# Weighted values two groups behind, two rings of weighted scores, and row maxima sent and fetched in separate groups, in an attention and MLP kernel

## The chip, the cores and the metric

The kernel runs on one core of a Trainium2 chip. The metric is the device time of one execution in microseconds. Before the change it is 1613.96 us, the median of three runs (1613.82 to 1614.4). One execution was profiled: it took 1613.86 us, and its span on the engines, from the first instruction to the last, is 1612.1 us.

## The reference

The input is 2048 rows of 512 numbers. A layer norm, attention with 32 heads of 16 columns each, a projection, a residual; then a second layer norm and an MLP of width 1792 with SiLU, and a residual again:

```python
scores = jnp.einsum("bhqd,bhkd->bhqk", q, k) * scale
p = _softmax(scores, axis=-1)
o = jnp.einsum("bhqk,bhkd->bhqd", p, v)
...
h = x + _A_ref(_layernorm(x, axis=-1), A_wqkv, A_wo)
h2 = h + _B_ref(_layernorm(h, axis=-1), B_w1, B_w2)
```

## The kernel before

**Stages.** Until about 180 us the kernel normalizes the rows and makes queries, keys and values. Then comes the attention as one long loop (line 1392), and after it, from about 1500 us, the end of the last block's MLP. The 2048 query rows are four blocks of 512. An *item* is four heads of one block, 32 items in all, and has 16 *groups*; a group takes 128 keys for the four heads, so there are 512 groups.

**A group.** For each of its four heads (numbered k = 0 to 3) TensorE makes scores of 128 keys by 512 queries in PSUM (`ps<-qs,ks`), ScalarE weighs them, which is the exponential, into an SBUF tile of the pool `bp` (`pt<-ps`, L111), and TensorE multiplies the values into them (`ps<-pt,va`, function `values`): four matmuls of 17 columns side by side in the array, each as two instructions since the tiles are float32, so eight instructions, a *burst* in this text. The four sums lie in one PSUM bank, `pv`. When the 16 groups of an item are summed, `finish_item` (line 881) has ScalarE copy the bank out (`pvs`, for items from 8 on) before the next item's first burst may write it, and starts a chain of DMAs and GpSimd work that divides by the sums.

**Maxima.** The softmax needs each row's maximum beforehand. A *maximum* is one matmul of 128 queries by 512 keys (`ps<-ks,qs`) and one VectorE reduction of 512 columns (`mx<-ps`, L307). Sixty-four of them make an item complete. The maxima run ahead of the scores by a plan, `maxima(g)` at line 1361, which says how many fall into each group. `at["done"]` counts those issued.

**What becomes of finished maxima.** `found_maxima` (line 399) chooses. If the item's scores begin more than FAR = 5 groups later, GpSimd reduces the rest and three ticks later (a tick, line 384, is the start of a group) `place_far` (line 344) has VectorE transpose the result (`mt<-ns`) and issues six DMAs on SyncE's queue: four that send it to DRAM (`md<-mt`) and two that fetch it back as two rows of the query tile (`qs<-md`), which wait for the four. Otherwise the late way is taken: VectorE and GpSimd reduce at once, and two groups later `place_max` (line 357) transposes on TensorE, copies on VectorE and issues two DMAs (`qs<-mn`). In such a group one maximum fewer is planned. The scores of an item read these rows, so they wait for the DMA.

**The two kinds of group.** For three of the four blocks the MLP of the block before is computed beside the attention: after the items 8, 16 and 24 begin, some groups hold the output projection, the second layer norm and its transpose (function `output`, line 1224), and then 112 groups in a row (the last time 110) are *beside* groups. These are the groups 146 to 257, 274 to 385 and 402 to 511. In the transpose, four tiles `g` of two buffers are filled by ScalarE and GpSimd or VectorE, and each is sent by a transposing DMA on SyncE's queue (`hts<-g`, line 131).

In a beside group, `beside_products` (line 1178) interleaves half-height matmuls of the MLP (64 of 128 rows) with the group's scores and maxima on the other 64 rows, so that two run at once. It works on pairs of groups: in the even group G it makes the scores of the heads k = 0 and 2 of both G and G+1, and in the odd group G+1 those of k = 1 and 3 of both. Six halves are done in a group. When a chain of halves is complete, always in an odd group, ScalarE copies its bank out (`g<-ps,factors`), between the second and the third exponential. In beside groups three PSUM banks take turns for scores (four otherwise) and three for maxima.

**Lag.** At the end of group g the values of group g - 2 are multiplied in, but in beside groups those of group g - 1 (line 1464: `while done <= g - (1 if g in beside else LAG)`). All weighted scores share one ring of 12 tiles. Every engine runs its instructions in the order in which this program issues them, DMAs of SyncE's queue included.

**Plan in beside groups.** Four maxima are planned in a beside group, five while `64 + 4 * (g + LEAD) > at["done"]` with LEAD = 7 (3 in the last 110), line 1368.

Of the kernel before, what the change touches and what calls it, by code (L numbers as in the profile page):

```python
# [10 lines left out]
F32 = mybir.dt.float32  # L11
# [9 lines left out]
P = 128  # L21
# [6 lines left out]
FC = F // P  # L28
# [18 lines left out]


LAG = 2
PTS = 12  # L50

RING = 5

# [20 lines left out]

LOOK = 5

LEAD = 7


BESIDE_V = [(0, 0), (0, 0, 4, 4)], [(2, 4), (4, 4, 4, 4)], [(6, 6), (6, 6, 6, 6)]  # L80
# [9 lines left out]
def attention_mlp_kernel(ctx: ExitStack, tc: tile.TileContext, x, wqkv, wo, w1, w2, out):  # L90
# [253 lines left out]
    def place_far(piece):  # L344

        i, _ = piece
        mt = small.tile([P, 32], F16, name="mt")
        dve("transpose", mt, split.pop(piece))
        issue = dma
        for b in range(4):  # L350
            issue(md[i, :, 32 * b:32 * b + 32], mt[32 * b:32 * b + 32, :])
        for j in range(2):
            issue(qs[i % RING][64 * j + 48:64 * j + 50].rearrange("r a n -> r (a n)"),
                md[i, 16 * j:16 * j + 16, :].rearrange("(r q) n -> r (q n)", r=2))
        placed.add(piece)

    def place_max(piece):

# [99 lines left out]

    groups = ITEMS * KC
    pts, den = {}, {}  # L460

    def pt_tile(name, dtype=F32):
        return bp.tile([P, 512], dtype, tag="pt", name=name)

    def scores(g, k, kind="st"):

        i = g // KC
        a, j, c = head(g, k)
        assert piece_of(i, a) in placed
        ps = bank(kind)  # L470
        mm(ps, ks[i % RING][64 * j:64 * j + 64, a, c * P:(c + 1) * P], qs[i % RING][64 * j:64 * j + 64, a, :],
           start=True, stop=True)

        def weigh():
            pts[g, k] = pt_tile("pt")
            return act("activation", pts[g, k], ps, AF.Exp, scale=qk_f)

        return weigh
# [117 lines left out]
    def project_qk(b, n, beside={}, scale=False):  # L596

        g, key = divmod(n, 2)
        cols = slice(key * D + g * P, key * D + (g + 1) * P)
        ps = bank()  # L600
        if b == 0 and g == 0:
            cols = slice(key * P, (key + 1) * P)
            wh, wl, xh, xl = wqk0_h, wqk0_l, xth0, xtl0
        else:
            wh, wl, xh, xl = wqk_h, wqk_l, xth[b], xtl[b]
        weave(product(ps, lambda c: wh[:, c, cols], lambda c: wl[:, c, cols],
                      lambda c: xh[:, c, :], lambda c: xl[:, c, :], DC),
              {k: n if callable(n) else (lambda n=n: burst(n)) for k, n in beside.items()})
        sh = xp.tile([P, 512], F16, name="sh")
        sl = xp.tile([P, 512], F16, name="sl", bufs=2)  # L610
        if scale:

            t = scaled[b % 2]
            act("mul", t, ps, 1 / (16.0 * LN))
            act("copy", sh, t)
            pool("tensor_tensor", sl, t, sh, ALU.subtract)
        else:
            act("mul", sh, ps, qk_0)
            dve("scalar_tensor_tensor", sl, ps, qk_0, sh, op0=ALU.mult, op1=ALU.subtract)
        d = (kd if key else qd)[g * P:(g + 1) * P, :, b * 512:b * 512 + 512]  # L620
        hs, ls = (slice(0, 3, 2), 1) if key else (slice(0, 2), 2)
        dma(d[:, hs], sh[:, None, :].to_broadcast([P, 2, 512]))
        dma(d[:, ls], sl)
# [185 lines left out]

    pb.close()  # L810
    cpool = ctx.enter_context(tc.tile_pool(name="cpool", bufs=1, side="right"))
    bp = ctx.enter_context(tc.tile_pool(name="bp", bufs=PTS, side="right"))
    first_scores = [(g, m ^ (g % 2)) for g in range(LAG) for m in range(4)]

    def begin_scores(n):
# [15 lines left out]
    for g in range(1, NG // 2):  # L831
        for m, (b, key) in enumerate([(b, 1) for b in range(NB)] + [(b, 0) for b in range(NB)]):
            tick()
            if g == 1 and m < 2:
                fixed_rows(2 + m)
            n = 8 * g + m - 12
            square_rest(n + 24)
            if n == 15:
                measure_rest()
            if n == 18:  # L840
                set_factors()
            beside = {BESIDE_A1[m]: 6} if g == 1 and m < len(BESIDE_A1) else BESIDE_A
            if n >= 18:
                beside = BESIDE_T[n - 18]
            project_qk(b, 2 * g + key, beside, True)
            for load, i, h in loads.get(n, ()):
                load(i, h)
    pa.close()
# [141 lines left out]
    def parts_of(w):  # L990
        return w.bitcast(F16).rearrange("p (s n) -> p s n", s=2)
# [69 lines left out]
        low(halves[t][:, 1], rows, halves[t][:, 0], "pool" if t < 3 else "dve")  # L1061

    def gate(ps, engine="dve"):
        g, parts = zp.tile([P, 512], F32, name="g"), parts_of(pt_tile("gh"))
        act("activation", g, ps, AF.Silu, scale=h_f)
        act("mul", parts[:, 0], g, g_s)
        if engine == "pool":
            pool("tensor_scalar", g, g, g_s, 1.0, op0=ALU.mult, op1=ALU.mult)
            low(parts[:, 1], g, parts[:, 0], "pool")
        else:  # L1070
            dve("scalar_tensor_tensor", parts[:, 1], g, g_s, parts[:, 0], op0=ALU.mult, op1=ALU.subtract)
        return parts[:, 0], parts[:, 1]
# [178 lines left out]
    def finish_last(pending):  # L1251
# [85 lines left out]
        for f in range(FC):  # L1337
# [11 lines left out]
            if f > 1:  # L1349
                second(b, acc, *waiting.pop(0))  # L1350
        last_seconds(b, acc, [gate for _, *gate in waiting])

    marks = [KC * (8 * b + 1) for b in range(1, NB)]

    beside = {g for m in marks for g in range(m + 2, min(groups, m + 2 + 4 * FC + 4 * FC))}
    fixed = {**{8 * KC * b + c: 3 + (MORE[c - OUTPUT - 1] if OUTPUT < c <= OUTPUT + 4 else 0) for b in range(1, NB) for c in range(2, KC + 2)},
             **{g: 4 for g in beside}}
    before = [sum(n for x, n in fixed.items() if x < g) for g in range(groups + 1)]
    free = [sum(x not in fixed for x in range(g)) for g in range(groups + 1)]

    def maxima(g):

        i, c = divmod(g, KC)
# [28 lines left out]
    for g in range(groups):  # L1392
        tick()
        i, c = divmod(g, KC)
        at["group"], at["next"] = None, g
        if g in marks:
            begin_mlp(i // 8 - 1)
        if (g in beside) != (g - 1 in beside):
            lay_out(st=range(3 if g in beside else 4))
        if i + RING - 1 < ITEMS and 6 <= c < 14:  # L1400
            (load_k if c % 2 else load_q)(i + RING - 1, c // 2 - 3)
        if g < DC:
            w = raw_tile()
            dma(w, wo[g * P:(g + 1) * P, :])
            soon(8, split_wo, g, w)
        f, c4 = divmod(g - SPLIT, SPACING)
        if c4 == 0 and 0 <= f < 2 * FC:
            kind, f = ("w1", "w2")[f % 2], f // 2
            soon(4, split_weights, kind, f, load_raw(kind, f))
        if i in FIRSTS:  # L1410
            b, n = i // 8 - 1, c - OUTPUT
            if c < 4:
                load_rows(b, c)
            if c == 9:
                wanted.extend(weights_of)
                if i == FIRSTS[-1]:
                    wanted.extend((("w1", 0), ("w1", 1), ("w1", 2), ("w2", 0)))
            if c in (9, 12, 13, 14, 15):
                want(1)
            if c in (3, 4):  # L1420

                split_rows(b, c - 3, slice(0, DC - 1))
            if n == 0:
                for t in range(2):
                    split_rows(b, t, slice(DC - 1, DC))
        if i == LAST:
            if c < 4:
                load_rows(NB - 1, c)
            if 5 <= c < 9:

                split_early(c - 5)
        if g == 1:
            dve("memset", pv, 0.0)
        at["group"] = g
        n = maxima(g)

        if g in beside:
            beside_products(g, n)
        else:
            half = 1 - head(g, g % 2)[1]  # L1440
            j = next_item()
            more = len(todo[j, half]) - len(todo[j, 1 - half]) if j < ITEMS else 0
            slots = range(n)
            if n == 3 and more < 0:
                slots = range(1, 4)
            if n == 2 and more > 0:
                slots = 0, 2
            for m in range(4):
                k = m ^ (g % 2)
                if (g, k) not in pts:  # L1450
                    scores(g, k)()
                if m in slots:
                    one_max(1 - head(g, k)[1])
        if found_at["step"] < at["step"]:
            finish_rest()
        for j in late.pop(at["step"], ()):

            place_max(j)
        if i in FIRSTS and OUTPUT + 1 < c < OUTPUT + 4:

            split_rows(i // 8 - 1, c - OUTPUT)
        if i in FIRSTS and c > OUTPUT:
            output(i // 8 - 1, c - OUTPUT - 1)
        while done <= g - (1 if g in beside else LAG):
            values(done)
            done += 1
    assert at["done"] == END
# [33 lines left out]
```

## Time and profile before

| what | value |
|---|---|
| median of three runs | 1613.96 us (1613.82 to 1614.4) |
| profiled execution | 1613.86 us, span 1612.1 us |
| TensorE granted clock | 0.993 of full speed |
| TensorE busy | 1586.0 us, 98% |
| VectorE busy | 1377.2 us, 85% |
| ScalarE busy | 1240.0 us, 77% |
| GpSimd busy | 577.8 us, 36% |

PE is TensorE's matmuls, PEld its weight loads, DVE is VectorE, ACT ScalarE, POOL GpSimd, SP SyncE; a q behind the name is the engine's own sequencer, which issues DMAs. Times are microseconds from the start of the span. A tile is written `out<-in`. In the list of instructions in order of time, the columns are start, length, engine, line, operation, tiles, shapes and count; in brackets stands how long the engine was idle before it and what ended that. The chain of waits is followed back from the last instruction and printed as start, length, what. In the table by stretch, a row has the stretch, its length, and the busy time and count of PE, PEld, DVE, ACT and POOL. The ends of matmuls are modelled, so the starts are what is read here.

### The profile page before, as it was taken

What the parts mean: (1) busy time and instruction counts of PE and PEld (TensorE: products, weight loads), DVE (VectorE), ACT (ScalarE), POOL (GpSimd) and SP (SyncE); (2) the same over time, 40 slices, a digit from 0 to 9 for tenths busy, and PEclk for the clock granted to TensorE, in tenths of its full rate; (3) what the DMA queues carried; (4) which work ended last, traced back from release to release, by engine and by line L of the source; (5) the groups of instructions that cost most, each with busy time, mean ns of one, the idle gap of its engine ahead of it and who ended that gap; (6) DMA issues with size and microseconds to landing.
All of it is one profiled execution on the core that took longest, in us unless ns stands there. A gap on an engine that the chain in (4) does not pass through costs nothing.

```text
span 1612.1 us, 31239 instructions
## 1 busy us (share of the span) xinstructions
PE 1586.0 (98%) x11485; PEld 520.1 (32%) x11485; DVE 1377.2 (85%) x2199; ACT 1240.0 (77%) x2404; POOL 577.8 (36%) x861
## 2 busy tenths in 40 slices
PE   9999999999999999999998999999999999999999
PEld 6434222222222333333322333333322333332354
DVE  7999999999998999999887999999887989995232
ACT  5545799999976888877776888877767888778632
POOL 6743544454342454311252454311252444212100
PEclk9999999999999999999999999999999999999999
DMA  6666433334223111444333211444333221334322
GB/s 217 169 179 213 132 85 87 108 113 116 85 62 89 54 49 42 127 133 130 105 73 88 54 47 48 127 128 131 104 79 88 65 58 36 87 102 143 118 82 76
DMA packets 136045, 162.49 MB, mean 101 GB/s; under 512 B 42992, under 2 KB 79920, under 8 KB 135892
## 3 DMA queue, kind: packets, MB, share of 16 engines
q1 hardware_dynamic: 131140, 151.98, 33.7%
q10 hardware_dynamic: 4752, 8.52, 1.9%
q8 instruction: 90, 1.47, 0.4%
q14 instruction: 63, 0.52, 0.1%
HBM read 126.69 MB, written 24.84 MB: 94 GB/s over the span
## 4 chain that ended last, share of the span: by engine, by line
PE 88%; DVE 8%; ACT 1%; DMA 1%; issue 1%; POOL 0%; SPq 0%; POOLq 0%; ACTq 0%; DVEq 0%
PE ps L97 87%; DVE mx L307 6%; DVE mx L305 1%; PE ps L100 1%; ACT pt L111 1%; DMA hts<-g 1%; ACT g L111 0%; POOL wv_l L104 0%; DMA w<-w2d 0%; SPq L127 0%; DVE pvs L121 0%; DVE g L121 0%; DVE st L121 0%; DVE ot L121 0%; DVE ks L121 0%
## 5 line engine op out<-in xcount | busy, mean ns | idle before, releaser
L307 DVE TENSOR_REDUCE mx<-ps 128x1 f32<-128x512 f32 x1842 | 1146.5, 683 | 96.7 <-PE ps L97 72.8
L111 ACT ACTIVATE pt<-ps 128x512 f32<-128x512 f32 x2048 | 1053.7, 605 | 208.9 <-PE ps L97 201.2
L97 PE MATMUL ps<-ks,qs 48*128 48x512 f16 x2048 | 680.4, 382 | 7.6 <-DVE mx L307 4.0
L97 PE MATMUL ps<-qs,ks 64*128 64x512 f16 x2048 | 644.4, 380 | 11.8 <-ACT pt L111 11.7
L97 PE MATMUL ps<-pt,va 128*17 128x512 f32 x4096 | 565.5, 601 | 0.5 <-DVE pvs L121 0.3
L97 PE MATMUL ps<-hts,w 64*128 64x512 f16 (+2 forms) x1212 | 285.1, 372 | 0.3
L97 PE MATMUL ps<-w,gates 64*128 64x512 f16 x1008 | 246.0, 378 | 0.3
L97 PEld LDWEIGHTS <-ks 64*128 64x128 f16 x2048 | 177.5, 95 | 212.5 <-issue 170.1
L97 PEld LDWEIGHTS <-qs 48*128 48x128 f16 x2048 | 169.2, 95 | 78.3 <-issue 35.3
L97 PEld LDWEIGHTS <-w 64*128 64x128 f16 (+1 forms) x1212 | 102.0, 95 | 236.8 <-ACT pt L111 105.6
L104 POOL TENSOR_TENSOR ri<-rc,minus 128x16 f32<-128x16 f32 x31 | 90.7, 2926 | 204.4 <-DMA rc<-dn 204.4
L97 PEld LDWEIGHTS ps<-pt,va 128*17 128x17 f32 x4096 | 84.5, 95 | 221.3 <-issue 207.5
L97 PEld LDWEIGHTS <-gates 64*128 64x128 f16 x1008 | 82.1, 94 | 218.4 <-ACT pt L111 119.7
L305 DVE TENSOR_REDUCE mx<-ps 128x2 f32<-128x1024 f32 x103 | 119.2, 1218 | 4.1 <-PE ps L97 3.5
L104 POOL TENSOR_SCALAR t<-t,factors 128x512 f32<-128x512 f32 x42 | 29.0, 691 | 198.7 <-ACT t L111 198.7
L111 ACT ACTIVATE g<-ps,factors 128x512 f32<-128x512 f32 x68 | 46.9, 690 | 42.6 <-PE ps L97 42.6
L104 POOL TENSOR_TENSOR ot<-ot,g 128x512 f32<-128x512 f32 x12 | 15.2, 1266 | 162.5 <-ACT g L111 162.5
L111 ACT ACTIVATE ks<-ps 128x512 f32<-128x512 f32 x30 | 17.9, 597 | 48.9 <-PE ps L97 43.0
L121 DVE SCALAR_TENSOR_TENSOR gh<-g,factors,gh 128x512 f16<-128x512 f32 x14 | 10.5, 752 | 52.1 <-ACT gh L111 52.1
L104 POOL TENSOR_TENSOR t<-t,g 128x512 f32<-128x512 f32 x42 | 53.5, 1275 | 3.5
L104 POOL TENSOR_TENSOR sl<-ks,sh 128x512 f16<-128x512 f32 x30 | 34.6, 1156 | 50.5 <-ACT sh L111 35.7
L104 POOL TENSOR_TENSOR mx<-mx 128x32 f32<-128x32 f32 x52 | 12.4, 239 | 109.2 <-DVE mx L307 102.6
(161 smaller groups left out, 1065.9 us busy)
## 6 DMA issues: line engine op xcount, KB each, us to landing
w<-w2d SPq DMA_DIRECT2D x182, 256.0 KB
ks<-kd SPq DMA_DIRECT2D x120, 192.0 KB
w<-w1d SPq DMA_DIRECT2D x56, 256.0 KB
ks<-in_B_w_dram ACTq DMA_DIRECT2D x28, 256.0 KB
w<-in_B_w_dram SPq DMA_DIRECT2D x28, 256.0 KB
qs<-qd SPq DMA_DIRECT2D x128, 48.0 KB
kd<-sh SPq DMA_DIRECT2D x16, 256.0 KB
qd<-sh SPq DMA_DIRECT2D x16, 256.0 KB
```

The costliest lines, as they stand in the source:

```text
L97: return tc.keep_in_program_order(nc.tensor.matmul(*a, **k))
L100: tc.keep_in_program_order(nc.tensor.transpose(*a))
L104: tc.keep_in_program_order(getattr(nc.gpsimd, op)(*a, **k))
L111: ins = getattr(nc.scalar, fn)(*a, **k)
L121: pin(getattr(nc.vector, fn)(*a, **k))
L305: pin(nc.vector.tensor_reduce(of, space[:, n:n + 2, :], axis=AX.X, op=ALU.max))
L307: pin(nc.vector.tensor_reduce(of[:, j:j + 1], space[:, n, :], axis=AX.X, op=ALU.max))
```

## The change

At the end of every group the values of two groups earlier are multiplied in, in beside groups too. The ring of 12 tiles becomes two rings, of 6 and 8 tiles; a tile comes from the second ring for odd groups where the group is a beside group, and for the heads k = 2 and 3 elsewhere. LEAD goes from 7 to 5. The four DMAs that send the maxima go out one group after the transpose, and the two that fetch them back one group after that; only ahead of the attention do they still follow at once. The plan's tables (`marks`, `beside`, `fixed`, `before`, `free`) move up in the file so that `scores` can use `beside`, and a local name is changed from `beside` to `bursts`.

```diff
 LAG = 2
-PTS = 12
+PTS = 6, 8
...
-LEAD = 7
+LEAD = 5
...
@@ place_far
         dve("transpose", mt, split.pop(piece))
-        issue = dma
-        for b in range(4):
-            issue(md[i, :, 32 * b:32 * b + 32], mt[32 * b:32 * b + 32, :])
-        for j in range(2):
-            issue(qs[i % RING][64 * j + 48:64 * j + 50].rearrange("r a n -> r (a n)"),
-                md[i, 16 * j:16 * j + 16, :].rearrange("(r q) n -> r (q n)", r=2))
-        placed.add(piece)
+
+        def out():
+            for b in range(4):
+                dma(md[i, :, 32 * b:32 * b + 32], mt[32 * b:32 * b + 32, :])
+
+        def back():
+            for j in range(2):
+                dma(qs[i % RING][64 * j + 48:64 * j + 50].rearrange("r a n -> r (a n)"),
+                    md[i, 16 * j:16 * j + 16, :].rearrange("(r q) n -> r (q n)", r=2))
+            placed.add(piece)
+
+        if at["attention"]:
+            soon(1, out)
+            soon(2, back)
+        else:
+            out()
+            back()
...
-    def pt_tile(name, dtype=F32):
-        return bp.tile([P, 512], dtype, tag="pt", name=name)
+    def pt_tile(name, second, dtype=F32):
+        return bp.tile([P, 512], dtype, tag=f"pt{second}", name=name, bufs=PTS[second])
...
         def weigh():
-            pts[g, k] = pt_tile("pt")
+            pts[g, k] = pt_tile("pt", g % 2 if g in beside else k // 2)
             return act("activation", pts[g, k], ps, AF.Exp, scale=qk_f)
...
     def gate(ps, engine="dve"):
-        g, parts = zp.tile([P, 512], F32, name="g"), parts_of(pt_tile("gh"))
+        g, parts = zp.tile([P, 512], F32, name="g"), parts_of(pt_tile("gh", 1))
...
-        while done <= g - (1 if g in beside else LAG):
+        while done <= g - LAG:
             values(done)
             done += 1
```

More of the change, by code (lines that the diff above doesn't have):

```diff
@@ L460, in attention_mlp_kernel @@
     pts, den = {}, {}
-    def pt_tile(name, dtype=F32):
-        return bp.tile([P, 512], dtype, tag="pt", name=name)
+    marks = [KC * (8 * b + 1) for b in range(1, NB)]
+    beside = {g for m in marks for g in range(m + 2, min(groups, m + 2 + 4 * FC + 4 * FC))}
+    fixed = {**{8 * KC * b + c: 3 + (MORE[c - OUTPUT - 1] if OUTPUT < c <= OUTPUT + 4 else 0) for b in range(1, NB) for c in range(2, KC + 2)},
+             **{g: 4 for g in beside}}
+    before = [sum(n for x, n in fixed.items() if x < g) for g in range(groups + 1)]
+    free = [sum(x not in fixed for x in range(g)) for g in range(groups + 1)]
+    def pt_tile(name, second, dtype=F32):
+        return bp.tile([P, 512], dtype, tag=f"pt{second}", name=name, bufs=PTS[second])
     def scores(g, k, kind="st"):
@@ L811, in attention_mlp_kernel @@
     cpool = ctx.enter_context(tc.tile_pool(name="cpool", bufs=1, side="right"))
-    bp = ctx.enter_context(tc.tile_pool(name="bp", bufs=PTS, side="right"))
+    bp = ctx.enter_context(tc.tile_pool(name="bp", bufs=1, side="right"))
     first_scores = [(g, m ^ (g % 2)) for g in range(LAG) for m in range(4)]
@@ L841, in attention_mlp_kernel @@
                 set_factors()
-            beside = {BESIDE_A1[m]: 6} if g == 1 and m < len(BESIDE_A1) else BESIDE_A
+            bursts = {BESIDE_A1[m]: 6} if g == 1 and m < len(BESIDE_A1) else BESIDE_A
             if n >= 18:
-                beside = BESIDE_T[n - 18]
-            project_qk(b, 2 * g + key, beside, True)
+                bursts = BESIDE_T[n - 18]
+            project_qk(b, 2 * g + key, bursts, True)
             for load, i, h in loads.get(n, ()):
@@ L1351, in finish_last @@
         last_seconds(b, acc, [gate for _, *gate in waiting])
[L1353 to L1359, printed above, removed]
     def maxima(g):
```

## The prediction

> **What bounds the kernel now.** First the page: who is busy, and who ends the chain of waits.
>
> ```profile
> span 1612.1 us, 31239 instructions
> PE 1586.0 (98%) x11485; PEld 520.1 (32%) x11485; DVE 1377.2 (85%) x2199; ACT 1240.0 (77%) x2404; POOL 577.8 (36%) x861
> PE 88%; DVE 8%; ACT 1%; DMA 1%; issue 1%; POOL 0%; SPq 0%; POOLq 0%; ACTq 0%; DVEq 0%
> ```
>
> TensorE's order sets the end; VectorE does for 8%. A TensorE that is busy 98% seems to leave nothing to win. But ends of matmuls are modelled, so a matmul that is held back looks busy. Second, therefore, the matmuls of the values alone, by stretch (first plain groups, then the three runs of beside groups), and third two bursts of eight in order of time with the exponential that ran there.
>
> ```profile
> 181.00:444.00 263.00, 134.52 (x1024) 16.87 (x1016) 0.00 (x0) 0.00 (x0) 0.00 (x0) 1.00 0.37 104
> 499.95:804.60 304.65, 124.95 (x891) 20.18 (x888) 0.00 (x0) 0.00 (x0) 0.00 (x0) 1.00 0.32 90
> 862.30:1167.00 304.70, 125.01 (x892) 20.18 (x888) 0.00 (x0) 0.00 (x0) 0.00 (x0) 1.00 0.32 90
> 1223.00:1500.00 277.00, 114.94 (x824) 18.42 (x816) 0.00 (x0) 0.00 (x0) 0.00 (x0) 1.00 0.30 86
> ...
> 699.82 0.59 ACT L111 ACTIVATE pt<-ps 128x512 f32<-128x512 f32 x1
> 700.28 1.22 PE L97 MATMUL ps<-pt,va 128*17 128x512 f32 x8
> 701.43 0.39 PE L97 MATMUL ps<-w,gates 64*128 64x512 f16 x1
> 702.75 0.37 PE L97 MATMUL ps<-qs,ks 64*128 64x512 f16 x1
> 703.06 1.05 PE L97 MATMUL ps<-pt,va 128*17 128x512 f32 x8
> 704.04 0.39 PE L97 MATMUL ps<-w,gates 64*128 64x512 f16 x1
> ```
>
> Eight matmuls take 134.52 / 128 = 1.051 us where values follow two groups behind. In the three beside runs they take 124.95 / 111.4 = 1.122, 125.01 / 111.5 = 1.121 and 114.94 / 103 = 1.116. The single bursts say why: 1.05 in one group, 1.22 in the other. The long one stands at the end of an odd group, where the even group's values are taken. It needs the exponentials of k = 1 and 3, made in that same odd group, and the one at 699.82 ends at 700.41, after the burst began at 700.28. To the next matmul it is 701.43 - 700.28 = 1.15 us, against 704.04 - 703.06 = 0.98. So 0.17 us of waiting for ScalarE, drawn as busy, is in nearly every second beside group.
>
> **The change part by part.** *Values two behind.* At the end of group G+1 the values of G-1 are then taken, whose exponentials ended a group earlier. All bursts should take 1.05: saved are 111.4 x 0.071 + 111.5 x 0.070 + 103 x 0.065 = 22.4 us, and about 0.7 for the last dozen groups: **-23.1**. The sum of matmuls is the same; the tail has two bursts instead of one behind the last group.
>
> *Two rings.* When the even group's exponentials of k = 0 and 2 are written, the first ring holds four tiles of G-2 and these two: six. In the odd group the second holds four of G-1 and four of G+1: eight. Six and eight are just enough, and the burst that frees a tile stands ahead of the score whose exponential fills it: 0.
>
> *The copy of the sums.* `finish_item` moves from the end of the even group 16n to the end of the odd group 16n+1, and its copy on ScalarE now stands between the exponentials of that group and the next. ScalarE around group 177 (from 584.98 to 587.82):
>
> ```profile
> 585.11 0.58 ACT L111 COPY pvs<-ps 128x512 f32<-128x512 f32 x1
> 585.72 1.08 ACT L111 ACTIVATE pt<-ps 128x512 f32<-128x512 f32 x2
> 586.69 0.69 ACT L111 ACTIVATE g<-ps,factors 128x512 f32<-128x512 f32 x1
> 587.26 2.79 ACT L111 ACTIVATE pt<-ps 128x512 f32<-128x512 f32 x5
> ...
> 702.08 2.08 ACT L111 ACTIVATE pt<-ps 128x512 f32<-128x512 f32 x4 [0.69 <-PE ps L97]
> ```
>
> The odd group also holds the copy of a finished MLP chain (0.69). Its exponentials start at 0.74, 1.2, 2.28 and 2.75 after the group's start; the last ends at 3.37. The copy of 0.6 then ends at 3.97, while the next group's first exponential is due at 2.63 + 0.65 = 3.28 (702.08 - 701.43 = 0.65): 0.69 late. The fourth score of a group reuses the first one's bank, of three: it stands 702.75 - 701.43 = 1.32 after the start, and the first exponential ends at 1.25, so 0.07 is to spare and 0.62 is lost. Chains of the first MLP product end every fourth group, which meets 16n+1 in groups 161, 177, 193 and their like in each run, nine times: **+5.6**. Without the chain's copy the lateness is about 0.09 and the loss 0.02, nine times: **+0.2**. From both sides: 0 if PSUM's turns absorb it, 11 if all 18 lose the 0.62. I take the row's reading. Where a beside run ends (groups 257 and 385) the copy falls among exponentials that TensorE already waits for:
>
> ```profile
> 804.10 1.10 ACT L111 ACTIVATE pt<-ps 128x512 f32<-128x512 f32 x2
> 805.24 0.39 PE L97 MATMUL ps<-qs,ks 64*128 64x512 f16 x2 [0.52 <-ACT pt L111]
> ```
>
> It adds its 0.6 twice: **+1.2** (0 to 1.2).
>
> *LEAD from 7 to 5.* A group with five maxima is bound by VectorE:
>
> ```profile
> 500.36 3.08 DVE mx L307 x5
> 498.00:804.00 306.00, 305.11 (x2467) 100.69 (x2467) 282.65 (x462) 250.56 (x483) 100.75 (x153) 1.00 0.32 90
> ```
>
> It takes 3.08 us against 704.04 - 701.43 = 2.61 with four. I followed line 1368 through all groups by hand: groups with five were 11, 11 and 5 in the three runs and become 2, 13 and 9, since eight maxima fewer are done ahead and the next run starts with that debt. Three fewer: 3 x 0.47 = **-1.4**. The items 17, 18 and 25 are now complete five groups or fewer ahead (groups 267, 283, 395) and take the late way.
>
> *Maxima sent and fetched later.* SyncE's queue and the chain of waits where the second layer norm is transposed:
>
> ```profile
> 837.80 1.16 POOL L104 TENSOR_TENSOR g<-w,g 128x512 f16<-128x512 f32 x1 [0.46 <-ACT g L111]
> 840.70 1.84 DVE L307 TENSOR_REDUCE mx<-ps 128x1 f32<-128x512 f32 x3
> 840.80 2.44 SPq L127 DMA_DIRECT2D md<-mt  x4
> 844.30 0.52 SPq L127 DMA_DIRECT2D qs<-md  x2
> 845.69 1.25 SPq L131 DMA_TRANSPOSE hts<-g  x1
> 845.69 3.89 DMA hts<-g
> 849.66 0.62 ACT L111 CAST g<-w 128x512 f16<-128x512 f32 x1 [5.22 <-DMA hts<-g]
> 850.83 0.58 PE L97 MATMUL ps<-qs,ks 64*128 64x512 f16 x1 [4.41 <-ACT pt L111]
> ...
> 1212.60 0.58 PE L97 MATMUL ps<-qs,ks 64*128 64x512 f16 x1 [3.76 <-ACT pt L111]
> ...
> 479.18 0.32 SPq L127
> 480.47 1.42 DMA md<-mt
> 483.42 3.60 DMA hts<-g
> 488.27 0.58 PE L97 MATMUL ps<-qs,ks 64*128 64x512 f16 x1 [2.49 <-ACT pt L111]
> ```
>
> The second transposing DMA has its tile at 838.96 but stands in SyncE's queue behind the maxima's six DMAs, and goes at 845.69. ScalarE's next `g` waits for it to land, the exponentials queue behind that, and TensorE idles 4.41 us. In the second and third such place (items 17 and 25) the late way now puts two DMAs there, behind a small VectorE copy after two reductions: 840.70 + 1.23 + 0.15 = 842.1, two issues 0.52, so the transpose goes at 842.6, 3.1 us earlier; the third place the same, less its shorter queue, 2.9. In the first (item 9) send and fetch move behind the transposes of the next group. The transpose then goes at 477.4 and the old stall is gone, but the fetch stands behind the last transpose, whose tile VectorE can finish at about 484.9: issue 1.25 to 486.1, two fetches to 486.6, landing about 1.4 later (as `md<-mt`) at 488.0. The scores of item 9 were due at 485.8, so TensorE waits until 488.1, nearly as long as before. What is won is that VectorE has no backlog then: I take 2. Together **-8.0**; from both sides -10.7 (all three idles gone) and 0.
>
> Elsewhere the fetch in beside groups comes late. The maxima of an item are complete at 16n-6 instead of 16n-8, the transpose is at 16n-3, the send at 16n-2, the fetch at 16n-1, the first score at 16n. From transpose to score there are 3 x 2.63 = 7.9 us. Four issues (2.44), landing (1.42), two issues (0.52) and landing (1.4) are 5.8: 2.1 to spare, **0**. But two groups' weight loads may now go out between them:
>
> ```profile
> 1475.88 2.82 DMA w<-w2d
> ```
>
> One of these ahead costs 2.82 - 2.1 = 0.7 at 13 items, 9 us; below nothing it can't be. By the Trainium skill ("DMA: Bandwidth & Descriptors", Queues, rings and completion order) each DMA engine takes descriptors in ring order, so the small fetch would start behind the loads issued ahead of it; no row here shows how far it is held, and the sum by it is the second rival's.
>
> Sum: -23.1 + 5.6 + 0.2 + 1.2 - 1.4 - 8.0 = -25.5. The profiled execution's 1613.86 (its span and 1.8 around it, 0.1 under the median) becomes **1588.4**.
>
> **The rivals.** *VectorE becomes the bound.* It is busy 282.65 of 306 us in the first run; with 8 us less in that run it would be 95%. If its short waits ahead of reductions don't shrink, about half of the 23.1 stays: 1588.4 + 11.5 = 1600. For: groups with five already wait for it. Against: four reductions are 4 x 0.617 = 2.47 of 2.61.
>
> *The rows of maxima come back too late* (the slower side). Place: the first score of the 13 items 10 to 16 and 19 to 24. With two loads ahead the fetch lands 2 x 2.82 - 2.1 = 3.5 us late, 46 us in all, and the time is 1634; it decides from 25.5 / 13 = 2.0 us an item. For: the margin is one group where it was three. Against: SyncE often stands ahead of TensorE, so the fetch may go before its group.
>
> *The change doesn't do what it says*: the long burst has another cause than the exponential, and stays; then 1588.4 + 23.1 = 1611.5, which is no change by measurement. Against: the end at 700.41 fits the wait.
>
> **How the numbers follow.** Forecast 0.75, with its own range of 1580 to 1598 (transposes -2.7 or +8.0, copies -5.8 or +5.4); VectorE 0.10; rows late 0.09; no effect 0.06. Low end: 1588.4 - 2.7 - 5.8 - 1.2, about 1578. High end: forecast with 8.0 and 9 of the unknown costs, 1606, which takes in the first rival. A measurement here can't tell less than 0.2%, 3.2 us, from no change. Faster: forecast, VectorE and a small part of the late rows, 0.86; same 0.06; slower 0.08.
>
> **What would show it.** Bursts of 1.05 us in all beside groups, by the values' busy time over their count. Five reductions in 24 groups. TensorE's idle before 850 near 1 us; before 488 about 2.5, but released by `qs<-md`. In group 178 and its like a fourth score 0.6 late. Wrong it would be if VectorE takes the idle, or if TensorE waits for `qs<-md` where items begin.

## The result and the profile after

The changed kernel takes 1586.45 us, the median of four runs (1584.89 to 1586.9), against 1613.89 before, measured beside it: a ratio of 0.9829, with a 95% interval of 0.9812 to 0.9846. The forecast was 1588. The profiled execution took 1586.9 us with a span of 1585.1, which is 27.0 less than the 1612.1 of before.

First the page of the changed kernel: busy times, the chain of waits by engine, and the group of the values' matmuls. After it the same group in the kernel before.

```profile
span 1585.1 us, 31197 instructions
PE 1561.1 (98%) x11488; PEld 502.2 (32%) x11488; DVE 1376.3 (87%) x2202; ACT 1234.7 (78%) x2404; POOL 573.6 (36%) x843
PE 84%; DVE 8%; ACT 3%; issue 1%; POOL 1%; DMA 1%; SPq 0%; ACTq 0%; POOLq 0%; DVEq 0%
L97 PE MATMUL ps<-pt,va 128*17 128x512 f32 x4096 | 542.4, 602 | 0.5 <-DVE pvs L121 0.3
```

```profile
L97 PE MATMUL ps<-pt,va 128*17 128x512 f32 x4096 | 565.5, 601 | 0.5 <-DVE pvs L121 0.3
```

TensorE is busy 98% in both, and its busy time is 24.9 us shorter with three matmuls more (the transposes of the late way). The 4096 matmuls of the values alone cover 565.5 - 542.4 = 23.1 us less, although the mean of one is as long as before (602 and 601 ns). So this part of the gain lies in how the matmuls of a burst stand to each other, and the share of busy time does not show it. By stretch, again plain groups first and then the three runs of beside groups:

```profile
181.00:444.00 263.00, 134.40 (x1024) 16.82 (x1016) 0.00 (x0) 0.00 (x0) 0.00 (x0) 1.00 0.38 104
497.40:795.60 298.20, 118.49 (x904) 14.98 (x904) 0.00 (x0) 0.00 (x0) 0.00 (x0) 1.00 0.34 93
846.00:1148.00 302.00, 117.91 (x896) 14.86 (x896) 0.00 (x0) 0.00 (x0) 0.00 (x0) 1.00 0.34 92
1201.00:1480.00 279.00, 109.63 (x832) 13.95 (x832) 0.00 (x0) 0.00 (x0) 0.00 (x0) 1.00 0.31 88
```

A burst now takes 118.49 / 113 = 1.049, 117.91 / 112 = 1.053 and 109.63 / 104 = 1.054 us, as in plain groups (134.40 / 128 = 1.050).

Then the three places where the second layer norm is transposed. The first (item 9), by the chain of waits and TensorE's list in order of time:

```profile
485.40 0.30 SPq L127
485.75 1.65 DMA qs<-md
487.45 7.14 PE ps L97 x32
...
487.45 0.60 PE L97 MATMUL ps<-qs,ks 64*128 64x512 f16 x1 [2.72 <-DMA qs<-md]
```

TensorE idles 2.72 us where it idled 2.49. But it waits for the fetch of the maxima now, and no longer for ScalarE. The second and third (items 17 and 25), SyncE's queue at item 17 and TensorE's idle time at both:

```profile
828.66 1.39 SPq L127 DMA_DIRECT2D qs<-mn  x2
830.16 1.26 SPq L131 DMA_TRANSPOSE hts<-g  x1
834.49 0.37 PE L97 MATMUL ps<-qs,ks 64*128 64x512 f16 x1 [1.97 <-ACT pt L111]
...
1188.66 0.37 PE L97 MATMUL ps<-qs,ks 64*128 64x512 f16 x1 [1.96 <-ACT pt L111]
```

The two DMAs of the late way (`qs<-mn`) stand ahead of the second transposing DMA where six stood, and the idle times fall from 4.41 and 3.76 to 1.97 and 1.96. One score later, TensorE waits 0.46 us more at both, for VectorE.

### The profile page after: what moved, and what is told of

It reads as the page before. It is cut to its first block, busy times and chain, and to the rows that moved or that the text cites. A ratio compares the mean times of both kernels' runs of the same rounds, so it can differ in the third digit from the quotient of the medians.

```text
span 1585.1 us, 31197 instructions
## 1 busy us (share of the span) xinstructions
PE 1561.1 (98%) x11488; PEld 502.2 (32%) x11488; DVE 1376.3 (87%) x2202; ACT 1234.7 (78%) x2404; POOL 573.6 (36%) x843
## 4 chain that ended last, share of the span: by engine, by line
PE 84%; DVE 8%; ACT 3%; issue 1%; POOL 1%; DMA 1%; SPq 0%; ACTq 0%; POOLq 0%; DVEq 0%
PE ps L97 84%; DVE mx L307 5%; ACT pt L111 2%; DVE mx L305 1%; PE ps L100 1%; DMA hts<-g 0%; SPq L127 0%; ACT pvs L111 0%; DVE st L121 0%; POOL rs L104 0%; DMA ks<-in_A_x_dram 0%; ACT g L111 0%; POOL g L104 0%; POOL ri L104 0%; DVE w L121 0%
## 5 line engine op out<-in xcount | busy, mean ns | idle before, releaser
L97 PE MATMUL ps<-pt,va 128*17 128x512 f32 x4096 | 542.4, 602 | 0.5 <-DVE pvs L121 0.3
L97 PEld LDWEIGHTS ps<-pt,va 128*17 128x17 f32 x4096 | 68.5, 95 | 214.3 <-issue 208.9
```

The source lines that it names most:

```text
L97: return tc.keep_in_program_order(nc.tensor.matmul(*a, **k))
```

## The experiments

**One part at a time.** The change has three parts: the values two groups behind with their two rings, LEAD, and the later DMAs. Three kernels each make one of them alone; a fourth leaves LEAD out of the whole.

Values two groups behind and two rings alone:

```diff
-PTS = 12
+PTS = 6, 8
...
-        while done <= g - (1 if g in beside else LAG):
+        while done <= g - LAG:
```

> The kernel before with values two groups behind everywhere and the two rings of weighted scores, alone: LEAD stays 7 and the maxima are sent and fetched at once, as before. Theory (the long bursts wait for the exponential of k = 3): all bursts of beside groups take 1.05 us and 23.1 us go; ScalarE's copy of the sums, now behind an odd group's exponentials, costs 0.41 us at nine items as in the changed kernel's trace, 3.7 us; TensorE's idle before items 9, 17 and 25 stays at 2.5, 4.4 and 3.8 us. Time 1613.9 - 23.1 + 3.7 = 1594.5. Rival (VectorE becomes the bound): about half of it, near 1603. Rival (the bursts are long for another reason and it was the maxima's DMAs that gave the gain): 1612 to 1618.

Measured: 1594.31 us, ratio 0.9880 (0.9864 to 0.9897), 19.0 us less than the 1613.3 of before beside it. The matmuls of the values cover 541.6 us in place of 565.5:

```profile
L97 PE MATMUL ps<-pt,va 128*17 128x512 f32 x4096 | 541.6, 601 | 0.5 <-DVE pvs L121 0.3
```

So the long bursts come from the lag alone: the time is within 0.2 us of the theory, and the rivals' 1603 and 1612 are out.

LEAD 5 alone:

```diff
-LEAD = 7
+LEAD = 5
```

> The kernel before with LEAD 5 in place of 7, alone. Theory: groups with five maxima go from 27 to 24, 1.4 us; the items 17 and 25 take the late way, so the second transposing DMA is held by two DMAs in place of six, which gives 2.5 to 3 us at the one and 1.7 to 2.4 at the other; item 9 stays. Time 1613.9 - 5.5 to 7 = 1607 to 1608.5. Rival (LEAD is worth only its five-maxima groups): 1612.5. Rival (the late way costs TensorE a transpose and VectorE a copy and gives nothing): 1614 or more.

Measured: 1609.32 us, ratio 0.9975 (0.9965 to 0.9985), 4.0 us less where 5.5 to 7 were expected: nearest to the theory, and short of it. At item 17 TensorE idles as in the changed kernel:

```profile
845.22 0.37 PE L97 MATMUL ps<-qs,ks 64*128 64x512 f16 x1 [1.96 <-ACT pt L111]
```

The DMAs in later groups alone:

```diff
         dve("transpose", mt, split.pop(piece))
-        issue = dma
-        (four DMAs out, two back)
+        soon(1, out)
+        soon(2, back)
```

> The kernel before with the maxima sent one group after their transpose and fetched one group after that, alone; LEAD 7, values one behind in beside groups. Theory: before items 9, 17 and 25 the second transposing DMA is no longer held, but the fetch then stands behind the last transpose and TensorE waits for it instead: 1.7 us at item 9 as in the changed kernel, 1 to 2 at each of the others, nothing elsewhere since in beside groups the fetch has three groups to spare. Time 1609 to 1611. Rival (fetches that come a group later hold up scores at many items): 1616 or more. Rival (the wait only changes its name): 1613.9.

Measured: 1605.68 us, ratio 0.9954 (0.9937 to 0.9971), 7.6 us less: more than the 3 to 5 expected. TensorE's wait at item 17 does change its name, and is shorter than the 4.41 of before:

```profile
846.83 0.39 PE L97 MATMUL ps<-qs,ks 64*128 64x512 f16 x1 [2.75 <-DMA qs<-md]
```

The rest of the gain is not in this wait. From the first score of group 271 to that of 274, the time goes from 14.5 us before to 11.2: 1.7 us of that is the wait, and 1.6 is group 272, right behind it. Four groups right behind such a wait, by stretch: group 272 before, group 144 (item 9) in the changed kernel, and the groups 272 and 400 in this one. The number behind the five counts is the mean granted clock of TensorE.

```profile
850.83:855.63 4.80, 4.55 (x16) 0.57 (x16) 3.76 (x7) 3.66 (x7) 0.00 (x0) 0.50 0.47 109
487.45:491.11 3.66, 3.66 (x16) 0.58 (x17) 1.89 (x3) 2.06 (x4) 0.00 (x0) 0.50 0.17 67
846.83:849.99 3.16, 3.16 (x15) 0.46 (x17) 1.89 (x3) 2.06 (x4) 0.00 (x0) 0.59 0.16 59
1207.54:1209.50 1.96, 1.96 (x17) 0.44 (x17) 1.51 (x3) 1.54 (x4) 0.00 (x0) 1.00 0.34 123
```

Two things slow such a group. The first is a backlog: while TensorE waits for the fetch, ScalarE and VectorE work off what they have; while it waited for ScalarE, they had work left over (seven exponentials fall into the first stretch, four into the second). At the same half clock that is 4.80 against 3.66 us (4.80 or 4.81 at all three places before). The second is the clock: behind most of these waits it falls to half for 3.41 or 6.83 us, and the same group takes 3.66 us at half and 1.96 at full clock. In the profiled executions, apart from the last 3 us, the clock is at half for 20.5 us in all in the kernel before, as long in the changed kernel, and for 10.2 here. What decides between no such stretch, a short and a long one the runs don't show: at item 25 here none follows a wait of 2.76 us, at item 9 in the changed kernel a long one follows 2.72, and one short stretch here (at 1164.83) follows a wait of only 0.52. I had counted the backlog at item 9 (2 us) and not at the others, and the clock nowhere.

The changed kernel with LEAD 7:

```diff
-LEAD = 5
+LEAD = 7
```

> The changed kernel with LEAD 7 in place of 5. Theory: 27 groups with five maxima in place of 24, 1.4 us more; the items 17 and 25 go the long way with the fetch behind the last transpose, as item 9 does, so TensorE idles about 2.7 us there in place of 2.0, 1.4 us more together. Time 1586.5 + 2.8 = 1589. Rival (LEAD 5 was chosen since maxima complete too early otherwise hold tiles, or gives nothing): 1586.5. Rival (with LEAD 5 the fetch comes too late in beside groups): faster than 1586.

Measured: 1586.13 us, ratio 0.9830 (0.9813 to 0.9846), the same as with LEAD 5. The rival is right: on top of the other two parts LEAD is worth nothing that can be told. The starts of the groups' first scores in the two traces say how that comes out. At group 256 the kernel with LEAD 5 is 4.2 us ahead, since it has had nine five-maxima groups fewer; up to the first score of item 17 it gains 2.5 more by the late way, and ahead of item 25 another 1.4; and by group 416 it has paid all but 0.4 us back. Of that, 1.8 us goes in the two groups behind item 17's stall and 2.2 in those behind item 25's, where it has ScalarE's backlog and a half clock of 6.83 us, against the fetch and 3.41 us with LEAD 7. The other 3.7 us goes from group 274 to 385 and from 402 on, where LEAD 5 has six five-maxima groups more (6 x 0.47 = 2.8): these maxima are only put off.

The parts: 19.0 + 7.6 = 26.6 us for values and DMAs, of 27.2 in that kernel; with LEAD's 4.0 the sum would be 30.6, but LEAD and the DMAs free the same transposing DMA.

**The copy of the sums.** The forecast had ScalarE's copy, in groups that also copy an MLP chain out, delay the next group's fourth score. In the changed kernel, ScalarE and TensorE around the start of group 178 (579.70):

```profile
579.30 1.10 ACT L111 ACTIVATE pt<-ps 128x512 f32<-128x512 f32 x2
580.26 0.62 ACT L111 COPY pvs<-ps 128x512 f32<-128x512 f32 x1
580.72 2.13 ACT L111 ACTIVATE pt<-ps 128x512 f32<-128x512 f32 x4
...
581.43 0.37 PE L97 MATMUL ps<-qs,ks 64*128 64x512 f16 x1
```

The first exponential starts at 580.72 and the fourth score at 581.43, which is 581.43 - 579.70 = 1.73 after the start in place of 1.32: 0.41 late. The experiment puts the copy behind that exponential:

```diff
+        elif at["next"] + 1 in beside and not current:
+            copies.append(late_copy)   # copy, then the item's DMAs
+            return
...
                         weigh()
+                    while copies:
+                        copies.pop()()
```

> The changed kernel with ScalarE's copy of the sums, where an MLP chain was copied out in the same odd group, put behind the first exponential of the next group. Theory (the 0.41 us lost in group 162 and eight like it comes from that copy standing ahead of the first exponential, whose bank the fourth score waits for): the fourth score is on time and at most 0.15 us is left, where the next burst waits for the copy; 9 x 0.26 to 0.41 = 2.3 to 3.7 us less than the changed kernel, 1583 to 1584 for 1586.5, and in the trace group 162 takes no more than its neighbours. Rival (it is the copy of the chain, which stays): no change. Rival (the burst then waits for the copy as long as the score did): no change, with the wait at the burst.

Measured: 1585.39 us, ratio 0.9824 (0.9808 to 0.9841), not to be told from the changed kernel. The trace says why, ScalarE and TensorE around the same group, which starts at 577.32 here (the third of the exponentials is its first):

```profile
576.92 1.64 ACT L111 ACTIVATE pt<-ps 128x512 f32<-128x512 f32 x3
577.32 0.39 PE L97 MATMUL ps<-ks,qs 48*128 48x512 f16 x1
...
578.46 0.58 ACT L111 COPY pvs<-ps 128x512 f32<-128x512 f32 x1
578.64 0.37 PE L97 MATMUL ps<-qs,ks 64*128 64x512 f16 x1
579.09 1.05 PE L97 MATMUL ps<-pt,va 128*17 128x512 f32 x8
```

The fourth score is on time now, 578.64 - 577.32 = 1.32 after the start, so the cause was right. But the burst then waits for the copy to end at 579.04, which leaves 0.16 of the 0.41, and the exponentials behind the copy make the next group's fourth score 0.16 late. Nine times 0.09 is left, 0.8 us: the third reading, nearly. ScalarE has that work to do somewhere, and where it stands hardly matters.

The profiled execution is this kernel's fastest, 1583.41 us, and most of its lead is not the copy's: the slowest, 1586.84, had a granted clock of 0.994, this one 0.997. At item 9 TensorE waits 2.77 us for the fetch as in the changed kernel (2.72), but no half clock follows, and group 144 takes 1.96 us where it took 3.66 there:

```profile
487.38:489.34 1.96, 1.96 (x16) 0.44 (x17) 1.50 (x3) 1.54 (x4) 0.00 (x0) 1.00 0.67 248
```

**The fetch's margin.** Would rows of maxima that come back later hold up scores?

```diff
-            soon(2, back)
+            soon(3, back)
```

> The changed kernel with the maxima fetched two groups after they are sent in place of one, so at the start of the group whose scores read them. Theory (SyncE stands well ahead of TensorE, and the fetch has about two us to spare at 13 items): nothing or up to 0.5 us lost at each of them, 0 to 7 us, and up to 1.5 us at item 9: 1586.5 to 1594. Rival (rows of maxima that come back late were close to deciding): each of the 13 items loses a group, 2.6 us, or more, 34 us: about 1620.

Measured: 1587.88 us, ratio 0.9838 (0.9822 to 0.9855). At the 13 items nothing is lost: the distance between the two kernels' group starts changes by less than 0.1 us from group 152 to group 256, and again from 290 to 385. SyncE's queue ahead of item 13, whose first score is at 659.4 in the changed kernel, there and with the later fetch:

```profile
651.77 2.33 SPq L127 DMA_DIRECT2D md<-mt  x4
654.20 0.85 SPq L127 DMA_DIRECT2D w<-w2d  x2
655.25 0.55 SPq L127 DMA_DIRECT2D qs<-md  x2
```

```profile
652.19 2.38 SPq L127 DMA_DIRECT2D md<-mt  x4
654.67 0.85 SPq L127 DMA_DIRECT2D w<-w2d  x2
655.70 0.55 SPq L127 DMA_DIRECT2D qs<-md  x2
```

The order of the queue is the same in both, and of the 0.45 us by which the fetch is later, 0.42 are the whole kernel's delay there (its first score of item 13 is at 659.86). SyncE stands ahead of TensorE, and what the fetch waits for is the landing of the four DMAs. Measured from the item's first score, the fetch moves by 0.05 us or less at 11 of the 13 items and by 0.3 at the items 14 and 24. So the edit hardly made it later, and what a fetch that is really late would cost is not shown. Only at item 9 TensorE waits longer:

```profile
488.17 0.61 PE L97 MATMUL ps<-qs,ks 64*128 64x512 f16 x1 [3.71 <-DMA qs<-md]
```

**VectorE's room.** The first rival of the forecast was VectorE as the new bound. An instruction that nobody reads is added to each of the 334 beside groups:

```diff
         if g in beside:
+            dve("tensor_copy", idle_copy, ones[:, :16])
             beside_products(g, n)
```

> The changed kernel with one more VectorE instruction in each of the 334 beside groups, a copy of 16 columns whose result nobody reads. It measures how much room VectorE has left. Theory (four reductions take 2.47 us of a group of 2.61 to 2.65, so 0.14 to 0.18 is free, and the instruction takes about 0.1): 0 to 3 us more, 1586 to 1590. Rival (VectorE is now the bound): 0.1 x 310 groups, 31 us more, about 1617.

> The changed kernel with a copy of 128 columns in each beside group instead, about 0.2 us on VectorE. Theory (0.14 to 0.18 us is free in a group): the excess of 0.02 to 0.06 us in each of some 310 groups is lost, 6 to 19 us, 1592 to 1606. Rival (VectorE is now the bound): 62 us more, about 1650. Rival (VectorE has much room): 1587.

Measured: 1594.88 us with 16 columns (ratio 0.9883, 0.9854 to 0.9911) and 1599.21 with 128 (0.9910, 0.9881 to 0.9938), 8.4 and 12.8 us more than the changed kernel. VectorE in order of time, with 16 columns and with 128:

```profile
701.09 0.17 DVE L121 COPY idle_copy<-ones 128x16 f32<-128x16 f32 x1
701.30 2.49 DVE L308 TENSOR_REDUCE mx<-ps 128x1 f32<-128x512 f32 x4
```

```profile
702.62 0.22 DVE L121 COPY idle_copy<-ones 128x128 f32<-128x128 f32 x1
702.83 2.48 DVE L308 TENSOR_REDUCE mx<-ps 128x1 f32<-128x512 f32 x4
```

In these rows the next reduction starts 0.21 us after the copy in either. But with 16 columns VectorE stands idle for 0.04 of it (701.09 + 0.17 = 701.26). Where the reduction doesn't wait, it starts 0.10 us after the copy of 16 columns, as expected:

```profile
656.02 0.16 DVE L121 COPY idle_copy<-ones 128x16 f32<-128x16 f32 x1
656.12 0.69 DVE L308 TENSOR_REDUCE mx<-ps 128x1 f32<-128x512 f32 x1
```

After a copy of 128 columns it is 0.13 in 57 groups. The groups 160 to 255 by stretch, in the changed kernel, with 16 columns and with 128:

```profile
532.27:786.10 253.83, 253.69 (x2115) 81.21 (x2112) 239.24 (x391) 214.13 (x415) 85.59 (x130) 1.00 0.36 100
531.27:789.11 257.84, 255.53 (x2116) 81.19 (x2113) 251.98 (x488) 214.67 (x415) 85.78 (x130) 1.00 0.36 98
532.19:790.75 258.56, 255.61 (x2115) 81.25 (x2113) 256.32 (x488) 214.74 (x415) 85.90 (x130) 1.00 0.36 98
```

In the changed kernel VectorE is idle for (253.83 - 239.24) / 96 = 0.15 us of a group, with the copies for 0.06 and 0.02, and a group takes 2.64, 2.69 and 2.69 us. So VectorE had 0.15 us to spare in a group, as expected, and is not the bound of the changed kernel, but little more would make it that. The first expectation is missed although price and room were right: part of the room stayed unused, and why is not shown. The second is met. (Two runs each.)

**The stall at items 9, 17 and 25.** In the changed kernel with LEAD 7 the fetch stands behind the last transposing DMA at all three. This kernel transposes these maxima one group earlier, so that send and fetch go ahead:

```diff
-            soon(... CALM, place_far, piece)
+            soon(... CALM - (piece[0] - 1 in FIRSTS), place_far, piece)
```

> The changed kernel with LEAD 7, and the maxima of items 9, 17 and 25 transposed two groups after they are found in place of three, so that both the send and the fetch stand ahead of the transposing DMAs that they now follow. Theory (at items 9, 17 and 25 TensorE idles 2.7 us each since the fetch stands behind the last transposing DMA): the three idles go, 6 to 8 us less than the changed kernel with LEAD 7: 1578 to 1580 for 1586.1. Rival (the stall belongs to the chain of the second layer norm, and the fetch only names it): as much idle, now released by ScalarE or by the transposing DMA, 1586.

Measured: 1575.86 us, ratio 0.9761 (0.9745 to 0.9778): 10.3 us less than the changed kernel with LEAD 7, and more than the 6 to 8 expected. SyncE's queue at item 9:

```profile
474.99 1.90 SPq L127 DMA_DIRECT2D md<-mt  x4
477.92 1.25 SPq L131 DMA_TRANSPOSE hts<-g  x1
479.35 0.67 SPq L127 DMA_DIRECT2D qs<-md  x2
482.10 2.96 SPq L131 DMA_TRANSPOSE hts<-g  x2
```

The fetch stands between the second and the last two transposes, TensorE has no idle time of its own there up to the first beside group (0.51 us at 489.69), and the rival, a stall of the layer norm's own, is out. The idles were 2.7 to 2.8 us each, 8.3 together. The rest of the gain is in the two groups behind each of them. At item 9, with LEAD 7 and here:

```profile
487.52:494.39 6.87, 6.87 (x33) 1.29 (x34) 3.77 (x6) 4.21 (x9) 0.00 (x0) 0.57 0.09 33
484.40:489.92 5.52, 5.00 (x37) 1.13 (x35) 4.88 (x9) 4.95 (x11) 0.00 (x0) 1.00 0.48 101
```

At item 17 the two groups take 6.25 us with LEAD 7 and 6.30 here, at item 25 6.28 and 5.53; together that is 2.0 us. The granted clock is 1.000 in all four runs of this kernel, against 0.994 to 0.998 with LEAD 7: without the idles, no half clock follows. The five-maxima groups gain nothing: from group 147 to 257 the two kernels take 295.4 and 295.5 us. I had left the clock out.

Both repairs together:

> The changed kernel with LEAD 7, the early transpose at items 9, 17 and 25, and the copy of the sums behind the first exponential. Theory: the gains add, 8 to 12 us less than the changed kernel, 1575 to 1578. If only one of the two reasons holds, 1578 to 1584; if neither, 1586.

Measured: 1576.61 us, ratio 0.9766 (0.9749 to 0.9782), the same as the early transpose alone. The copy's 0.8 us is too little to be seen here.

## Why the prediction was right

The time, 1586.45 us, came out 2 us under the forecast of 1588.4 and inside its own range. By its steps:

*The bursts*, -23.1: the values' matmuls cover 23.1 us less, and the lag alone confirms it. Right in place and size. A burst is held by its latest column, and where the values are two groups behind, no column is late.

*The copy of the sums*, +5.6 and +0.2: the mechanism was right, the size not: 0.41 us each in place of 0.62, nine times 3.7. The mis-sized term is the copy's 0.6, its drawn length; between two exponentials it takes 580.72 - 580.26 = 0.46 from start to start. In the same way the copy does not wait for the drawn end of the last exponential: it starts 580.26 - 577.02 = 3.24 after the start of group 177, not 3.37. Without the chain's copy nothing is lost (0.2 forecast).

*The copy at the ends of the beside runs*, +1.2: nothing was lost, and the idle time at group 258 goes from 0.52 to 0.69 while the burst ahead of it became 0.17 shorter:

```profile
791.91 0.39 PE L97 MATMUL ps<-qs,ks 64*128 64x512 f16 x2 [0.69 <-ACT pt L111]
```

*LEAD*, -1.4: the count of five-maxima groups was right (24), and the late way of items 17 and 25 too. But it was summed as a gain of its own, and beside the later DMAs LEAD is worth 0 in all.

*The maxima's DMAs*, -8.0: the step at item 9 went as worked out. The transpose went at 477.3 (477.4), the fetch at 485.4 to 486.0 (486.6 at its end), TensorE started at 487.45 (488.1), and 1.7 us were won (2). The reason holds too: at the same half clock, the group behind the stall takes 3.66 us for 4.80. At item 17 the gain by the groups' starts is 3.0 (3.1) and at item 25 1.7 to 2.4 (2.9), as two issues of `qs<-mn` took 1.39 us and not 0.52. The sign named for item 17, an idle time near 1 us, did not come (1.97): 0.6 of the 3.0 us is won already in group 270, which takes 2.06 us for 2.66. What the step overlooked is that the long way would have done as well there. It also has no term for the half clock behind each stall; that cost it nothing, since the clock is at half for 20.5 us before and after.

The errors: copies 3.3 us too dear together, LEAD and DMAs about 2 us too good, and a few tenths at the tail. That they nearly cancel, so that the total is within 2 us, is luck.

*The rivals.* Rows too late: out. At item 13 the fetch does stand behind two weight loads, and no score is late. It goes 3.6 to 4.9 us ahead of the first score at the 13 items; with the 1.65 us that it took to land at item 9, the estimate for item 13 is a landing near 657.4 for a score at 659.4, about the 2 us of the forecast. By the ring order of the Trainium skill ("DMA: Bandwidth & Descriptors", Queues, rings and completion order), which has each DMA engine take descriptors in order, the fetch would start behind those loads. No run here shows how long it is held. VectorE: near, with 0.15 us free in a group, and not the bound. No effect: out.

## What to carry to other kernels

An engine's busy share hides waits inside a group of matmuls that run side by side: divide the time that such a burst covers by the count, in two stretches that differ in one thing, and look for two lengths. When a stall is removed, look at the group behind it too. Here it took 4.80 us where other engines had a backlog and the clock was at half, 3.66 at half clock alone and 1.96 with neither, so a stall costs more than its idle time. Read the granted clock of that stretch before naming another cause. The order of a queue sets what a transfer holds up: the gain was largest where a send and its fetch preceded the work that would hold them, and smaller where they were merely moved to a later place.

## What the runs showed of the hardware

Behind a wait of TensorE of 1.9 to 4.4 us, the granted clock mostly falls to half for 3.41 or 6.83 us, and the same group takes 3.66 us in place of 1.96. It does not fall behind every such wait: at item 9 it did after 2.72 us in the changed kernel and did not after 2.77 in the one with the later copy. A burst of eight matmuls side by side takes 1.22 us instead of 1.05 when one column's operand is late, and the difference is drawn as busy.

A reduction on VectorE follows a copy of 16 columns after 0.10 us, though the copy is drawn 0.16 long. An exponential of 512 columns is mostly drawn 0.59 to 0.62 us long, but ScalarE starts the next one 0.48 later (four cover 2.08 us where none waits); an exponential follows a copy of that size after 0.46 us at the nine places of the changed kernel. A transposing DMA occupies SyncE's queue 1.25 us to issue, where each of the four `md<-mt` takes 2.33 / 4 = 0.58.
